# Two three-bank score tiles that both lend a bank, one shared bank, and a second temporary for the scan's output weights

## Chip, cores and metric

The kernel runs on one core of one Trainium2 chip. The metric is the device time in microseconds of one execution; before the change three runs gave a median of 770.16 us (769.84 to 772.17).

## What is computed

Two independent blocks over 2048 positions of width 640, joined along the last axis. Block A is a diagonal complex state space: the input is projected to 640 complex states, a linear recurrence runs over the positions, and the states are projected back with a skip term. Block B is attention with 32 query heads of 20 columns that share one head of keys and one of values, without a mask, followed by an output projection.

```
# A
Bu = x @ B_bar.T            # complex, 2048 x 640
h[t] = Lam_bar * h[t-1] + Bu[t]
y = 2 * real(h @ C.T) + x * Dskip
# B
scores = (x wq)_h . (x wk) * 20**-0.5      # 32 heads, 2048 x 2048 each
o = softmax(scores) @ (x wv)
out = concat(y, o @ wo)
```

## The kernel before

Almost all of the time goes into the exponentials of the scores. The work is cut into units: one head, 512 queries and 128 keys give a score tile of 128 partitions by 512 columns, which is one PSUM bank. Four heads and 512 queries are a group (32 groups, 64 units each, 2048 units in all). A unit is made by PE (QK: `R<-QT,KT` or `B<-QT,KT`), turned into bf16 weights, and multiplied with the values and a column of ones into the bank PV (`PV<-P,VP` or `PV<-Pd,VP`).

The exponential has two makers. ACT reads a whole tile of several banks in one activation (L1263, P<-R). DVE takes single units: one instruction adds an offset and rounds to int16 (L1269, Pd<-B or Pd<-R), which as bits of bf16 approximates a power of two, and three shifted copies (L1274, over up to three units at once) correct it, so that a unit of DVE has four PV products where one of ACT's has one.

PSUM has eight banks. Before, tile R0 has three banks, tile R1 two, PV one, and two banks, B0 and B1 (tensor BB), are shared. ACT works on R0 and R1 in turn while PE fills the other. A unit for DVE goes to B0 or B1 or, with `lend`, to R0's third bank R0c; then R0's next tile has two banks. The shared banks also serve the background, each piece of which locks a bank from its first matmul until DVE has read it: the scan's input (thread sa: five matmuls, then L901), its output y (sy: 12 or 13 matmuls, L962), the dense Q (qt: five matmuls, L775, with the norm row at L800), and the output projection (proj: five matmuls, L1061).

The order on each engine is fixed when the program is built. A planner (`main`) holds a clock for each engine and modelled durations, gathers in every round the next operation of each thread and the next fill, exponential, DVE unit, shift and PV step, gives each its earliest start plus a bias, and issues the smallest. Small random choices of its thresholds (`vary`) change 64 times in the course, by the numbers in SEEDS. A fill is ordered ahead of a background matmul that would make it late (`t_fill`, with `after` for how late it may be). If PE would wait more than SPARE, the planner adds matmuls by zeros into PV that keep PE's clock up. `want_d` says whether a unit for DVE is wanted: DVE's backlog must be small, the bank free, and no background thread starved; lending ends when 40 units of the last group are taken (`t_left`).

The scan runs in units of 512 positions and 128 states (20 in all): L901 makes rotated inputs (tm), POOL adds them (uh, L917), DVE scans (L928), POOL rotates back (tm<-hh) and writes W (W<-tm), and PE turns W into y with the output weights CGre and CGim. Those weights are made once: the C matrices arrive by transposing DMAs in W's memory (Craw) and ostage; for each of ten products POOL multiplies five pieces into the temporary ctmp (L858), then DVE combines them (L860). Before, there is one ctmp, inside tm, and the scan's way back waits for all ten (`prog["c"]`). The dense part for 512 queries (L1011, OTd) reads the heads' outputs back from DRAM and normalises them.

P, ACT's output, is a ring of ten tile places with 25 units. The set-up (0 to about 22 us) makes K from four banks, of which it holds two while V is made (`rest`).

Of the kernel before, what the change touches and what calls it, by code (L numbers as in the profile page):

```python
# [243 lines left out]
class _Kernel:  # L244
    S, D, H, DH = 2048, 640, 32, 20
    NC, NQB, NKC, NGG = 5, 4, 16, 8
    BANKS = 2
    PIECES = "abcd"
    TILES, PTILES, DUNITS, DSHIFT, QRING = (3, 2), 10, 9, 3, 4
    SHIFTS = (0, 33, 65, 95)  # L250

# [3 lines left out]
    SPARE = 0.33  # L255
# [9 lines left out]
    SEEDS = (19006, 20002, 21006, 22006, 23001, 24003, 25001, 26002, 27008, 28003, 0, 30006, 31008, 32005, 33006,  # L265
# [28 lines left out]
    def alloc(self):  # L294
        S, NC = self.S, self.NC
        nc = self.nc
        self.R = [self.scope.enter_context(nc.psum_tensor(f"R{i}", [128, 512 * n], FP32))
                  for i, n in enumerate(self.TILES)]
        self.PV = self.scope.enter_context(nc.psum_tensor("PV", [128, 512], FP32))
        self.BB = self.scope.enter_context(nc.psum_tensor("B", [128, 512 * self.BANKS], FP32))  # L300
        self.B = [self.BB[:, 512 * i:512 * i + 512] for i in range(self.BANKS)] + [self.R[0][:, 1024:1536]]
        self.bkeys = [f"B{i}" for i in range(self.BANKS)] + ["R0c"]
        self.p.psum.update(["R0", "R0c", "R1", "R1b", "PV", *(f"B{i}" for i in range(self.BANKS))])
# [25 lines left out]
        self.sb("P", [128, self.PTILES * 5 // 2, 512], BF16)  # L329
# [7 lines left out]
        self.wq_raw = self.P[:].rearrange("p s n -> p (s n)")[:, 18 * 512:18 * 512 + NC * 640].rearrange("p (c n) -> p c n", c=NC)  # L337
# [24 lines left out]
        self.ctmp = self.tm[:].rearrange("p i n -> p (i n)").bitcast(FP32)[:, 1024:1664]  # L362
# [67 lines left out]
    def setup(self):  # L430
# [51 lines left out]
        pk = ["P7", "P8", "P9"]  # L482
# [23 lines left out]
        banks = [(K.R[1], 0, "R1"), (K.R[1], 512, "R1b"), (K.BB, 0, "B0"), (K.BB, 512, "B1")]  # L506
# [39 lines left out]
        for m, src, keys in ((0, K.R[1][:, 0:1024], ["R1", "R1b"]), (1, K.BB[:, 0:1024], ["B0", "B1"])):  # L546
# [270 lines left out]
    def scan_ops(self):  # L817
# [4 lines left out]
        sa, su, sr, sy, sc_ = [], [], [], [], []  # L822
        self.prog = prog = dict(x=0, a=0, u=0, s=0, r=0, y=0, w=0, c=0)
# [9 lines left out]
        ct = [f"tm{i}{h}" for i in (4, 5, 6) for h in self.PIECES]  # L833
# [14 lines left out]
        for c in range(NC):  # L848
            for i, nm in ((0, "cre"), (1, "cim")):
                sc_.append(self.dma(K.Craw[c][:, i, :], t[nm][:, 128 * c:128 * (c + 1)], f"craw{c}{i}",  # L850
                                    writes=[f"Craw{c}{i}"] + ([f"ostage{i}"] if c == 4 else []), tr=True, kb=160))
        for c in range(NC):
            cr, ci = K.Craw[c][:, 0, :], K.Craw[c][:, 1, :]
            keys = [f"Craw{c}0", f"Craw{c}1", "sc"] + (["ostage0", "ostage1"] if c == 4 else ws)
            for (dst, x, y, gx, gy, op, nm) in ((K.CGre, cr, ci, GRE, GIM, ALU.subtract, "CGre"),
                                                (K.CGim, ci, cr, NGRE, NGIM, ALU.add, "CGim")):
                for i in range(0, 640, 128):
                    pool(lambda e, y=y, c=c, gy=gy, i=i: e.tensor_scalar(K.ctmp[:, i:i + 128], y[:, i:i + 128], sc[:, gy, c:c + 1],  # L858
                                                                         None, op0=ALU.mult), keys, [f"ct{i}"] + ct * (i == 0), 128)
                dve(lambda e, dst=dst, x=x, op=op, c=c, gx=gx: e.scalar_tensor_tensor(  # L860
                    out=dst[:, c, :], in0=x, scalar=sc[:, gx, c:c + 1], in1=K.ctmp, op0=ALU.mult, op1=op),
                    keys + ct + [f"ct{i}" for i in range(0, 640, 128)], [nm], 695)
        sc_[-1].done = lambda: prog.update(c=1)
# [16 lines left out]
        sx = [o for b in (1, 2, 3) for o in self.load_xa(b, lambda b=b: prog["y"] >= 4 * (b - 1), lambda b=b: prog.update(x=b))]  # L880
        return sc_, sy, sr, su, sa, sx
# [7 lines left out]
    def scan_in(self, ops, dve, b, c):  # L889
# [4 lines left out]
        for k, (nm, BT) in enumerate((("BTre", K.BTre), ("BTim", K.BTim))):  # L894
            h = Hold()
            for cd in range(NC):
# [5 lines left out]
                K.tm[:, 2 * k:2 * k + 2, :], bass.AP(tensor=K.BB, offset=512 * int(h.key[1]),  # L902
# [224 lines left out]
    def main(self):  # L1127
# [184 lines left out]
        while True:  # L1312
# [108 lines left out]
            if kind == "bg":  # L1421
# [5 lines left out]
                if o.free:  # L1427
                    owner[int(o.hold.key[1])] = None
# [102 lines left out]
```

## Time and profile before

| | us |
|---|---|
| median of three runs | 770.16 |
| the profiled execution | 770.28 |
| its span, first to last instruction | 768.6 |
| ACT busy in the span | 752.5 |
| DVE busy | 708.3 |
| PE busy (pipelined, ends modelled) | 704.8 |
| POOL busy | 446.0 |

The profile is one execution on the chip. Its page gives busy times by engine, the chain of work that ended last, and groups of instructions by line with output and input tile, count, busy time, mean duration, and the idle time before them with what ended it. All PE work is recorded at one helper line (L421), so PE is read by tiles. The granted clock (PEclk) is the share of full speed that the chip's throttle gave to PE.

### The profile page before, as it was taken

To read this page: it belongs to the slowest core of one execution; us is meant where nothing else is said; L and a number is where in the kernel's file an instruction comes from. 1 tells how busy PE (TensorE), PEld (TensorE's weight loads), DVE (VectorE), ACT (ScalarE), POOL (GpSimd) and SP (SyncE) were. 2 spreads that over 40 slices of the span, in tenths; PEclk is the share of its full clock that TensorE was granted. 3 is DMA by queue.
4 is the path that set the end of the run, shared out by engine and by line. 5 is a ranking of instruction groups with operands and counts; after the bars stand their busy time and mean duration, and the time that the engine had idled before them with its cause. 6 is when DMAs were issued, how large, how long until landed. Compare 5 with 4: busy or idle time off the path is not lost.

```text
span 768.6 us, 16664 instructions
## 1 busy us (share of the span) xinstructions
PE 704.8 (92%) x6538; PEld 213.4 (28%) x6538; DVE 708.3 (92%) x1236; ACT 752.5 (98%) x710; POOL 446.0 (58%) x867
## 2 busy tenths in 40 slices
PE   5799988888889999998889999988889999889998
PEld 2222222222222333322223323322223332223333
DVE  5599999999998999999997999999999789999986
ACT  8999999999999999999999999999999999999995
POOL 5612354579989931088997300199986469990040
PEclk9899999899999999999999999999999999999999
DMA  9366301000021100220002100040000201000020
GB/s 186 57 143 134 74 16 49 8 24 14 3 51 30 42 8 27 56 60 15 15 9 67 42 23 9 23 93 10 15 15 28 66 33 34 14 15 17 18 61 35
DMA packets 61179, 31.50 MB, mean 41 GB/s; under 512 B 41510, under 2 KB 61102, under 8 KB 61102
## 3 DMA queue, kind: packets, MB, share of 16 engines
q1 hardware_dynamic: 59606, 30.14, 15.9%
q8 instruction: 52, 0.85, 0.5%
q10 hardware_dynamic: 1496, 0.30, 0.2%
q14 instruction: 25, 0.20, 0.1%
HBM read 9.21 MB, written 12.69 MB: 28 GB/s over the span
## 4 chain that ended last, share of the span: by engine, by line
ACT 74%; PE 15%; DVE 9%; POOL 1%; DMA 1%; issue 1%; ACTq 0%; DVEq 0%; POOLq 0%
ACT P L1263 72%; PE R L421 5%; PE PV L421 5%; PE B L421 4%; DVE Pd L1274 4%; DVE Pd L1269 3%; DVE hh L928 1%; DVE tm L901 1%; POOL tm L858 1%; DMA WO<-in_B_wk_dram 1%; ACT cs L691 1%; ACT Pd L690 0%; ACT KT L538 0%; DVE CGre L860 0%; ACT L503 0%
## 5 line engine op out<-in xcount | busy, mean ns | idle before, releaser
L1263 ACT ACTIVATE P<-R 128x1024 bf16<-128x1024 f32 (+1 forms) x677 | 733.1, 1354 | 4.3 <-PE R L421 1.8
L421 PE MATMUL R<-QT,KT 32*128 32x512 bf16 (+1 forms) x1685 | 266.9, 389 | 48.6 <-ACT P L1263 37.1
L1269 DVE TENSOR_SCALAR Pd<-B 128x512 int16<-128x512 f32 x363 | 245.5, 682 | 19.4 <-PE B L421 17.0
L1274 DVE TENSOR_SCALAR Pd<-Pd 128x1536 int16<-128x1536 int16 (+2 forms) x513 | 260.2, 541 | 0.4
L421 PE MATMUL PV<-Pd,VP 128*32 128x512 bf16 x1744 | 256.9, 386 | 2.0 <-DVE OTr L1307 1.0
L421 PE MATMUL PV<-P,VP 128*32 128x512 bf16 x1612 | 253.3, 389 | 0.7 <-DVE OTr L1307 0.6
L917 POOL TENSOR_TENSOR tm<-hh,cs 128x128 bf16<-128x128 f32 x320 | 163.9, 533 | 17.7 <-DVE hh L928 8.3
L421 PEld LDWEIGHTS R<-QT,KT 32*128 32x128 bf16 (+1 forms) x1685 | 66.1, 91 | 301.0 <-ACT P L1263 271.0
L421 PE MATMUL B<-QT,KT 32*128 32x512 bf16 x363 | 141.0, 389 | 0.0
L917 POOL TENSOR_TENSOR uh<-tm 128x128 bf16<-128x128 bf16 x160 | 81.0, 527 | 97.6 <-DVE tm L901 93.7
L917 POOL TENSOR_TENSOR W<-tm 128x128 bf16<-128x128 bf16 x160 | 93.5, 608 | 49.4 <-PE B L421 45.3
L421 PEld LDWEIGHTS PV<-Pd,VP 128*32 128x32 bf16 x1744 | 60.1, 94 | 65.7 <-issue 40.5
L421 PEld LDWEIGHTS PV<-P,VP 128*32 128x32 bf16 x1612 | 58.1, 94 | 58.8 <-issue 46.6
L1011 POOL TENSOR_TENSOR OTd<-OTd,rwide 128x128 bf16<-128x128 bf16 x80 | 33.2, 443 | 60.0 <-DMA OTd<-o_rows 58.2
L1269 DVE TENSOR_SCALAR Pd<-R 128x512 int16<-128x512 f32 x73 | 49.9, 683 | 3.0 <-PE R L421 2.4
L901 DVE TENSOR_TENSOR tm<-B,cs 128x1024 bf16<-128x1024 f32 x40 | 48.5, 1213 | 1.0 <-PE B L421 0.6
L858 POOL TENSOR_SCALAR tm<-W,sc 128x128 f32<-128x128 bf16 x40 | 32.3, 821 | 27.5 <-DVE CGre L860 15.9
L421 PE MATMUL B<-CGre,W 128*128 128x384 bf16 (+1 forms) x160 | 46.4, 305 | 0.0
L421 PE MATMUL B<-CGim,W 128*128 128x384 bf16 (+1 forms) x160 | 45.5, 299 | 0.0
L928 DVE TENSOR_TENSOR_SCAN hh<-sc,hini,uh 128x512 f32<-128x512 f32 x30 | 40.7, 1358 | 0.0
L421 PEld LDWEIGHTS B<-QT,KT 32*128 32x128 bf16 x363 | 32.9, 91 | 0.0
L421 PE MATMUL B<-xaT,BTre 128*128 128x512 bf16 x100 | 30.1, 384 | 0.1
(149 smaller groups left out, 437.2 us busy)
## 6 DMA issues: line engine op xcount, KB each, us to landing
o_rows<-OTr SPq DMA_DIRECT2D x32, 128.0 KB, 1.7
QT<-q_rows SPq DMA_DIRECT2D x30, 128.0 KB, 2.2
q_rows<-Qd SPq DMA_DIRECT2D x16, 160.0 KB, 2.9
OTd<-o_rows SPq DMA_DIRECT2D x16, 160.0 KB, 3.4
out_dram<-ystage SPq DMA_DIRECT2D x16, 160.0 KB, 1.9
out_dram<-ostage SPq DMA_DIRECT2D x12, 160.0 KB, 1.8
P<-in_B_wq_dram SPq DMA_DIRECT2D x1, 800.0 KB, 5.6
WO<-in_B_wo_dram SPq DMA_DIRECT2D x4, 200.0 KB, 3.4
```

The source lines that it names most:

```text
L421: ins = e.matmul(o() if callable(o) else o, lhsT=l, rhs=r, start=st, stop=sp, skip_group_check=True, **kw)
L691: act(lambda e, c=c, b=b: e.activation(K.cs[:, c, :, :].rearrange("p i n -> p (i n)"), K.tri[:, 4 * b + 2:4 * b + 4, :].rearrange("p r n - ...
L858: pool(lambda e, y=y, c=c, gy=gy, i=i: e.tensor_scalar(K.ctmp[:, i:i + 128], y[:, i:i + 128], sc[:, gy, c:c + 1], None, op0=ALU.mult), key ...
L901: dve(lambda e, k=k, h=h: e.tensor_tensor(K.tm[:, 2 * k:2 * k + 2, :], bass.AP(tensor=K.BB, offset=512 * int(h.key[1]), ap=[[512 * self.BA ...
L917: put(lambda e, c0=c0, end=end: e.tensor_tensor(out[:, c0:end], a[:, c0:end], b[:, c0:end], op), reads, [writes + h], n, gate=None if i el ...
L928: dve(lambda e, ri=ri, ini=ini: e.tensor_tensor_scan(K.hh[:, ri, :], dec, K.uh[:, ri, :], ini, ALU.mult, ALU.add), ["sc", *(f"uh{ri}{h}" f ...
L1011: ops.append(Op("pool", lambda e, c=c, m=m: e.tensor_tensor(K.OTd[:, m, c], K.OTd[:, m, c], K.rwide[:, c], ALU.mult), rw + [f"OTe{dd}" for ...
L1263: return Op("act", lambda e: e.activation(dst, K.R[n % 2][:, 0:512 * size], ACT.Exp, scale=self.exp_scale), [f"R{n % 2}"] + ["R0c"] * (siz ...
L1269: return Op("dve", lambda e: e.tensor_scalar(K.Pd[:, 0, u, :], K.B[x][:, :], self.d_off, 0.0, op0=ALU.add, op1=ALU.max), [key], [f"Pd{u}_0 ...
L1274: return Op("dve", lambda e: e.tensor_scalar(K.Pd[:, i, a:b, :], K.Pd[:, 0, a:b, :], float(self.SHIFTS[i]), 0.0, op0=ALU.subtract, op1=ALU ...
```

## The change

PSUM becomes R0 (three banks), R1 (three banks), PV and one shared bank B0; R1 and B0 are one tensor, RB. Both tiles lend their third bank (R0c, R1c) to a unit of DVE. All of the background locks B0. P's ring hands out places unit by unit. The planner gets new random knobs: `prefer` lends even where B0 is free, `gap` spaces the blocks of one background thread, and the allowed lateness of a fill (`after`) goes by whether the tile that ACT has next is three wide. While the set-up's end runs and no PV matmul has begun, idle matmuls of the identity into B0 fill waits of PE over 0.25 us (WARM). The output weights get two temporaries in OTd and threads of their own (sl: loads, sk: POOL, sg: DVE); now only the writing of W and the dense part wait for them, the way back's rotations do not. The C loads stand ahead of wo's, and xa's second block waits for three of the ten products. All seeds are new.

```
-    BANKS = 2
+    BANKS = 1
-    TILES, PTILES, DUNITS, DSHIFT, QRING = (3, 2), 10, 9, 3, 4
+    TILE, PUNITS, DUNITS, DSHIFT, QRING = 3, 25, 9, 3, 4
-    SPARE = 0.33
+    SPARE, WARM = 0.33, 0.8
...
+        self.R0 = self.scope.enter_context(nc.psum_tensor("R0", [128, 512 * self.TILE], FP32))
+        self.RB = self.scope.enter_context(nc.psum_tensor("R1", [128, 512 * (self.TILE + 1)], FP32))
+        self.R = [self.R0, self.RB[:, 0:512 * self.TILE]]
+        self.B = [self.RB[:, 1536:2048], self.R[0][:, 1024:1536], self.R[1][:, 1024:1536]]
+        self.bkeys = ["B0", "R0c", "R1c"]
...
-        self.ctmp = self.tm[:].rearrange("p i n -> p (i n)").bitcast(FP32)[:, 1024:1664]
+        self.ctmp = self.OTd[:].rearrange("p c n -> p (c n)").bitcast(FP32).rearrange("p (i n) -> p i n", i=2)
...
+                    wide(lambda e, y=y, c=c, gy=gy, i=i, h=h: e.tensor_scalar(K.ctmp[:, h, i:i + 128], y[:, i:i + 128], sc[:, gy, c:c + 1],
+                                                                            None, op0=ALU.mult), keys, [f"ct{h}{i}"], 128,
+                         gate=lambda n=2 * c + h: prog["g"] >= n - 1 and prog["l"] > n // 2, done=(lambda n=2 * c + h + 1: prog.update(k=n)) if i == 512 else None)
+                cd(lambda e, dst=dst, x=x, op=op, c=c, gx=gx, h=h: e.scalar_tensor_tensor(
+                    out=dst[:, c, :], in0=x, scalar=sc[:, gx, c:c + 1], in1=K.ctmp[:, h, :], op0=ALU.mult, op1=op),
...
+        sx = [o for b in (1, 2, 3) for o in self.load_xa(b, lambda b=b: prog["y"] >= 4 * (b - 1) and prog["g"] > 2, lambda b=b: prog.update(x=b))]
...
-                   gate=lambda: prog["s"] > u and prog["c"], done=(lambda: prog.update(r=u + 1)) if i == 3 else None)
-        free = lambda: prog["y"] >= 4 * b
+                   gate=lambda: prog["s"] > u, done=(lambda: prog.update(r=u + 1)) if i == 3 else None)
+        free = lambda: prog["y"] >= 4 * b and prog["c"]
...
-        have = lambda: all(g in self.normed for g in range(self.NGG * qb, self.NGG * qb + (6 if qb == self.NQB - 1 else 8))) and (
+        have = lambda: self.prog["c"] and all(g in self.normed for g in range(self.NGG * qb, self.NGG * qb + (6 if qb == self.NQB - 1 else 8))) and (
...
-        self.lend = r.choice((0.5, 1.0))
-        self.open, self.first = r.choice((0.6, 0.7)), r.choice(("sy", "proj", None))
+        self.lend, self.prefer = r.choice((0.0, 0.5, 1.0)), r.choice((False, True))
+        self.gap = dict(sy=r.choice((0.0, 4.0, 8.0)), proj=r.choice((0.0, 4.0, 8.0)), sa=r.choice((0.0, 0.0, 4.0)),
+                        qt=r.choice((0.0, 0.0, 4.0)))
+        self.open, self.first = r.choice((0.6, 0.7, 0.8)), r.choice(("sy", "proj", None))
...
-            f = [i for i in range(2) if owner[i] is None]
-            if not f:
-                return None
-            return min(f, key=lambda i: p.begin("pe", (), (f"B{i}",)))
+            return 0 if owner[0] is None else None
...
-                    size, x = self.TILES[n % 2] - (n % 2 == 0 and owner[2] is not None), bank(None)
+                    lent = 1 + n % 2
+                    size, x = self.TILE - (owner[lent] is not None), bank(None)
                     d = want_d(g, t, n % 2)
-                    if not d and size == 3 and want_d(g, t, 0, True):
-                        size, d, x = 2, True, 2
+                    if (not d or self.prefer) and size == 3 and want_d(g, t, 0, lent):
+                        size, d, x = 2, True, lent
...
-                    t_fill = (t_fill, t_fill + self.after[n % 2])
+                    t_fill = (t_fill, t_fill + self.after[bool(tiles) and len(tiles[-1][1]) == 3])
...
+                    if o.lock and t_left() and not (name == "qt" and not self.qsent):
+                        bias += max(0.0, last.get(name, -99.0) + self.gap.get(name, 0.0) - p.clock["pe"])
...
+                if self.still and not any(begun[0]) and owner[0] in (None, "rest") and "B0" not in o.keys()[1]:
+                    while t - p.begin("pe", (), ("B0",)) > 0.25 and self.load(t) < self.WARM:
+                        self.go(self.mms([self.m1(K.B[0], K.ident[:, :], K.xbT[:, 0, 0:512], True, True)], ["ident", "xbT0"], ["B0"],
+                                         kind="zero"))
```

More of the change, by code (lines that the diff above doesn't have):

```diff
@@ new lines, in scan_ops @@
+        old = ["wk4", "wk_raw", "wv_raw", "onesrow", "selrow"] + ["veclim", "vecldt", "veclre", "vecdsk"]
+        sk, sg = [], []
+        cd = mk(sg, "dve")
+        wide = lambda fn, reads, writes, n, **k: sk.append(Op("pool", fn, reads, writes, occ=0.58, **k))
+        for c in range(NC):
+            cr, ci = K.Craw[c][:, 0, :], K.Craw[c][:, 1, :]
+            keys = [f"Craw{c}0", f"Craw{c}1", "sc"] + (["ostage0", "ostage1"] if c == 4 else ws)
+            for (dst, x, y, gx, gy, op, nm) in ((K.CGre, cr, ci, GRE, GIM, ALU.subtract, "CGre"),
+                                                (K.CGim, ci, cr, NGRE, NGIM, ALU.add, "CGim")):
+                h = int(nm == "CGim")
+                for i in range(0, 640, 128):
+                    wide(lambda e, y=y, c=c, gy=gy, i=i, h=h: e.tensor_scalar(K.ctmp[:, h, i:i + 128], y[:, i:i + 128], sc[:, gy, c:c + 1],
[3 more added lines that the diff above has]
+                    out=dst[:, c, :], in0=x, scalar=sc[:, gx, c:c + 1], in1=K.ctmp[:, h, :], op0=ALU.mult, op1=op),
+                    keys + [f"ct{h}{i}" for i in range(0, 640, 128)], [nm] + [f"OTd{i}{j}" for i in range(NC) for j in self.PIECES] * (c == NC - 1), 695,
+                    gate=lambda n=2 * c + h: prog["k"] > n, done=lambda n=2 * c + h + 1: prog.update(g=n, c=int(n == 2 * NC)))
@@ L847, in scan_ops @@
                 sc_.append(self.dma(dst, src, f"wo{j}{w}", reads=["WO4"], writes=[f"WO4_{j}{w}"], kb=200 if w else 50))
[L848 to L863, printed above, removed]
         for b in range(4):
@@ L1245, in fill_op @@
         def fill_op(n, out, d, x):
-            lst, reads, writes = [], set(), ([f"R{n % 2}"] if out else []) + ["R0c"] * (len(out) == 3)
+            lst, reads, writes = [], set(), ([f"R{n % 2}"] if out else []) + [f"R{n % 2}c"] * (len(out) == 3)
             units = list(out) + ([d] if d else [])
@@ L1345, in main @@
                             offer("fill", fill_op(n, [], d, bank(None)), 0.2, arg=([], d, bank(None)))
-            full = bool(tiles) and tile_left.get(tiles[0][0] - self.PTILES, 0) > 0
+            full = bool(tiles) and not vacant(len(tiles[0][1]))
             if tiles:
                 n, out = tiles[0]
-                if tile_left.get(n - self.PTILES, 0) == 0:
+                if not full:
                     offer("ex", ex_op(n, len(out)), 0.0)
@@ L1426, in main @@
                     since.pop(name, None)
+                    last[name] = p.clock["pe"]
                 if o.free:
```

85 lines of the change are left out of this document (46 added, 39 removed), and 8 rows, old and new, of the table SEEDS.

## The prediction

> **What bounds the kernel now.** I read the page first: the engines' busy times, then the chain that ended last.
>
> ```profile
> span 768.6 us, 16664 instructions
> PE 704.8 (92%) x6538; PEld 213.4 (28%) x6538; DVE 708.3 (92%) x1236; ACT 752.5 (98%) x710; POOL 446.0 (58%) x867
> ...
> PEclk9899999899999999999999999999999999999999
> ...
> ACT 74%; PE 15%; DVE 9%; POOL 1%; DMA 1%; issue 1%; ACTq 0%; DVEq 0%; POOLq 0%
> ```
>
> ACT is busy 98% of the span and is most of the chain. To see what else the span holds, I cut it at ACT's first and last exponential with the windows view (columns: length, then busy us and count of PE, PEld, DVE, ACT, POOL, then clock, DMA share, GB/s).
>
> ```profile
> 0.00:21.68 21.68, 12.65 (x43) 4.45 (x43) 12.82 (x29) 17.96 (x32) 11.81 (x30) 1.00 0.82 166
> 21.68:757.80 736.12, 684.72 (x6413) 204.68 (x6417) 691.00 (x1198) 731.87 (x679) 434.14 (x838) 0.99 0.15 37
> 757.80:768.60 10.80, 7.45 (x86) 4.30 (x78) 4.45 (x11) 2.65 (x4) 0.00 (x0) 1.00 0.17 61
> ```
>
> In the middle 736.12 us ACT works 731.87 and idles 4.25. All stalls together are thus worth 4.25 us; anything larger must come from ACT's own work: how many score units it gets, and how many instructions they are packed into. The groups with shapes kept apart show both (count, then busy us, mean ns).
>
> ```profile
> L1263 ACT ACTIVATE P<-R 128x1024 bf16<-128x1024 f32 x419 | 457.8, 1189 | 1.1 <-PE R L421 0.7 <-PE B L421 0.2
> L1263 ACT ACTIVATE P<-R 128x1536 bf16<-128x1536 f32 x258 | 418.3, 1621 | 3.2 <-PE R L421 1.2 <-PE B L421 1.1 <-PE PV L421 0.6
> L421 PE MATMUL PV<-P,VP 128*32 128x512 bf16 x1612 | 253.3, 389 | 0.7 <-DVE OTr L1307 0.6
> L421 PE MATMUL PV<-Pd,VP 128*32 128x512 bf16 x1744 | 256.9, 386 | 2.0 <-DVE OTr L1307 1.0 <-DVE Pd L1274 0.5 <-DVE Pd L1269 0.4
> L1269 DVE TENSOR_SCALAR Pd<-B 128x512 int16<-128x512 f32 x363 | 245.5, 682 | 19.4 <-PE B L421 17.0
> L1269 DVE TENSOR_SCALAR Pd<-R 128x512 int16<-128x512 f32 x73 | 49.9, 683 | 3.0 <-PE R L421 2.4
> ```
>
> ACT takes 1612 units of 512 columns (419 x 2 + 258 x 3 = 1612), DVE the other 363 + 73 = 436 (1744 / 4). Neighbouring exponentials overlap, so the two busy figures add to more than the union; that union is in the page's groups:
>
> ```profile
> L1263 ACT ACTIVATE P<-R 128x1024 bf16<-128x1024 f32 (+1 forms) x677 | 733.1, 1354 | 4.3 <-PE R L421 1.8
> L1274 DVE TENSOR_SCALAR Pd<-Pd 128x1536 int16<-128x1536 int16 (+2 forms) x513 | 260.2, 541 | 0.4
> ```
>
> One bank more costs 1621 - 1189 = 432 ns. With 677 tiles, 677a + 258 x 0.432 = 733.1, so a two-bank tile takes a = 0.918 us of ACT's time, of which two banks are 0.864. **A tile costs 0.054 us beyond its banks**; a unit costs 733.1 / 1612 = 0.455 us. These two prices carry the forecast: 0.054 for each tile less, about 0.45 for each unit that moves to or from DVE.
>
> **The change part by part.** *Wider tiles.* Both tiles now have three banks, and either lends its third to DVE; only one bank, B0, is left for the background (scan, projections, dense Q) and DVE's units together. A tile is two wide where it lends. So I need how many of DVE's units find B0 free. Its use by the background comes from the view of tile B (first and last start after the durations), and, for a projection, from the timeline (start, length):
>
> ```profile
> L421 PE MATMUL B<-CGre,W x160: 272/304/337, 267.4 to 740.7; 128*128 128x384 bf16 x80, 128*128 128x256 bf16 x80
> L421 PE MATMUL B<-xaT,BTre x100: 376/379/390, 55.1 to 657.1; 128*128 128x512 bf16 x100
> L901 DVE TENSOR_TENSOR tm<-B,cs x40: 1192/1212/1225, 57.3 to 661.2; 128x1024 bf16<-128x1024 f32 x40
> L962 DVE CAST ystage<-B x32: 408/474/558, 270.7 to 741.7; 128x384 bf16<-128x384 f32 x16, 128x256 bf16<-128x256 f32 x16
> ...
> 434.87 0.72 PE L421 MATMUL B<-WO,OTd 128*128 128x320 bf16 x4
> ...
> 436.45 0.48 DVE L1061 CAST ostage<-B 128x320 bf16<-128x320 f32 x1
> ```
>
> The first scan input holds a bank from 55.1 to 57.3 + 1.21, 3.4 us; the first half row of y from 267.4 to 270.7 + 0.56, 3.9; a projection from 434.87 to 436.93, 2.1. With 40 scan inputs, 32 y halves, 28 projections and 20 dense-Q blocks (five matmuls as a scan input and a shorter evacuation; I take 2.9), that is 136 + 125 + 59 + 58 = 378 us of the 725 us in which there are DVE units: an estimate that B0 is free 48% of the time. If DVE takes units at an even rate, 0.48 x 436 = 209 come from B0 and 227 are lent. With some 5 more two-wide tiles at the start there are 232, then (1612 - 464) / 3 = 383 three-wide ones: 615 tiles, 62 fewer, **-3.3 us**. The bounds: all 436 lent gives 441 two-wide, 243 three-wide, 7 tiles more, +0.4; none lent gives about 541 tiles, -7.3. I take the value from the free share.
>
> By the Trainium skill, ScalarE: Activation LUTs, section What ACT_TABLE_LOAD costs, an ACTIVATE with immediate operands takes 186 ns + 0.833 ns per column, and neighbours overlap by about 93 ns. By it a tile costs 93 ns beyond its banks and the 62 tiles 5.8 us; the rows above give 54 ns, and the measurement decides.
>
> *DVE's share.* DVE has three banks to draw from before (two shared, one lent) and after (one shared, two lent), but the background can no longer take two at once. What more units could come is in DVE's waits from 48 to 740 us (total, times, longest):
>
> ```profile
> DVE Pd L1269 <- PE B L421: 14.9, 53, 0.7
> DVE ystage L962 <- PE B L421: 7.2, 7, 2.1
> ...
> DVE Pd L1269 <- PE R L421: 2.4, 7, 0.7
> ```
>
> DVE stood 17.3 us waiting for a unit's scores. A unit costs DVE (245.5 + 49.9 + 260.2) / 436 = 1.27 us, so these waits are 13.6 units. With the 7.2 us before y's evacuation it would be 19.3, -8.8 us: the far end; the near one is 0, and what lies below nothing is the third rival. Nothing in the trace prices it more closely; I take a third of the 13.6, 4.5 units x 0.455 = **-2.1 us**. Against it: lending stops in the last group once 40 of its 64 units are taken, and there B0 is shared with the last projections. The timeline has six of DVE's units there, these first and last, out of two banks; I take two off (between none and six), **+0.9 us**.
>
> ```profile
> 746.83 0.69 DVE L1269 TENSOR_SCALAR Pd<-B 128x512 int16<-128x512 f32 x1 [0.34 <-PE B L421]
> ...
> 755.87 0.69 DVE L1269 TENSOR_SCALAR Pd<-B 128x512 int16<-128x512 f32 x1
> ```
>
> *Idle matmuls.* They keep PE's clock up in the set-up, into B0, until the first PV matmul:
>
> ```profile
> 28.00:34.00 6.00, 5.59 (x23) 1.11 (x27) 0.83 (x3) 5.83 (x6) 2.12 (x10) 0.52 0.05 5
> ...
> 22.07 2.18 PE L421 MATMUL PV<-WO,xbT 128*128 128x20 bf16 x80
> ...
> 24.62 9.21 ACT L1263 ACTIVATE P<-R 128x1536 bf16<-128x1536 f32 x8 [0.58 <-PE R L421]
> 34.45 14.20 ACT L1263 ACTIVATE P<-R 128x1536 bf16<-128x1536 f32 x13 [0.62 <-PE PV L421]
> ```
>
> The granted clock from 28 to 34 us is 0.52, and ACT's second gap there, 0.62 us at 34.45, stands behind PV matmuls on the slow clock. The first gap, at 24.62, has the fill behind V's 80 matmuls, before the clock falls, and stays. I take **-0.6 us**, between -1.2 (both gaps) and +0.4 (a 0.39 us matmul just ahead of a late fill). An idle matmul stands in PE's queue before whatever comes next, so if PE's wait is shorter than planned, the fill and then ACT wait for it.
>
> *Output weights of the scan.* The same 50 POOL and 10 DVE instructions; two temporaries in OTd in place of one in tm, so POOL need not wait for DVE to release it:
>
> ```profile
> POOL tm L858 <- DVE CGre L860: 20.3, 5, 8.4
> ...
> POOL tm L858 <- DVE CGim L860: 16.0, 4, 5.7
> ...
> 82.97 1.27 SPq L402 DMA_TRANSPOSE ostage<-in_A_C_re_dram  x1
> ...
> 162.75 8.10 POOL L917 TENSOR_TENSOR tm<-hh,cs 128x128 bf16<-128x128 f32 x16 [1.02 <-DVE CGim L860]
> ...
> 741.70 0.42 DVE L962 CAST ystage<-B 128x256 bf16<-128x256 f32 x1
> ...
> L421 PE MATMUL B<-WO,OTd x140: 297/299/310, 242.0 to 756.0; 128*128 128x320 bf16 x140
> ...
> L404 SPq DMA_DIRECT2D OTd<-o_rows x16: 316/436/465, 226.7 to 736.9; - x16
> ```
>
> The scan's way back starts at 162.75 us, behind those weights, and its last y leaves at 741.70, 16 us ahead of the last exponential's start. Starting earlier is worth nothing on ACT: 0. The ten C transposes move ahead of wo's loads on SP's queue (1.27 us each, 13 us). Q's rows share that queue but the planner prefers them, and wo is first used at 242 us, so this hides; without that preference a group's Q could come up to 13 us late. The new gate on xa's second block stands on the same queue; scan units of that block come after five of the first. OTd is first loaded at 227 us, so the dense part's new gate costs nothing while the weights finish before it.
>
> *P's ring, lateness by tile, gaps between background blocks, new seeds.* The ring holds the same 25 units. The rest moves waits about; all of ACT's waits left are 4.25 - 0.6 us, so I take 0, between -3.6 and +4.
>
> **Sum.** The profiled execution took 770.28 us (span 768.6 and 1.7 around it), 0.1 over the median of 770.16. 770.28 - 3.3 - 2.1 + 0.9 - 0.6 = **765.2 us**, 0.6% less.
>
> **The rivals.** *One: DVE's gaps close.* With a lendable bank at every fill DVE gains all 19.3 units, -8.8 in place of -2.1: 758.5. For it: ACT is the chain and its other costs are fixed. Against: DVE already works 691 of 736 us.
>
> *Two: nothing comes of it.* Background holds and preferred lending leave B0 hardly a unit, so two-wide tiles stay near 419, and DVE's count stays: 770.3 - 0.6 = 769.7. For it: 73 of 436 units are lent now, and the plan may lend even where B0 is free. It decides where over 400 units are lent.
>
> *Three, slower: DVE starves at the one shared bank.* A background block keeps B0 some 2 to 4 us, and a lent bank only comes free when DVE has read it; where DVE is behind, the next tile of the same kind is two wide and can't lend. Each unit that DVE loses costs ACT 0.455 us. Of the gains 3.3 + 0.6 = 3.9 us would be left, so it decides from 9 fewer units on (9 x 0.455 = 4.1); with 20 fewer it is 770.3 - 3.9 + 9.1 = 775.5. For it: B0 would be nearly always taken. Against: the two lendable banks are there at every fill.
>
> *Four, slower: PE's clock falls more often.* Fewer, wider tiles are fewer passes on PE. This happened once in the middle:
>
> ```profile
> 140.00:143.00 3.00, 2.15 (x19) 0.49 (x15) 3.00 (x7) 3.00 (x4) 2.73 (x5) 0.64 0.16 52
> 143.00:146.00 3.00, 3.00 (x21) 0.56 (x17) 2.17 (x6) 2.48 (x3) 0.51 (x1) 0.50 0.00 0
> 146.00:149.00 3.00, 3.00 (x28) 0.67 (x27) 2.98 (x6) 2.40 (x3) 0.36 (x1) 0.72 0.00 0
> ```
>
> PE works 2.15 of 3 us, the clock drops to 0.50, and ACT then idles 0.52 + 0.60 = 1.1 us. Seven such dips more would make it about 773. The planner still fills gaps over 0.33 us with matmuls into PV. The Trainium skill, TensorE: Matmul & The Clock Gate, section A second HAM failure mode: psum-queue depth-cycling, speaks for this rival: cycling through PSUM banks leaves short idle times in which the clock oscillates; the page's row of the clock above agrees so far that it fell in two stretches.
>
> **Chances.** The forecast's course (762 to 768) 0.50; one 0.18; two 0.12; three 0.14; four 0.06. A measurement of this kernel tells about 0.3%, 2.3 us, from no change. Faster by more: 0.50 + 0.18 = 0.68; within it: 0.12; slower: 0.20. For 8 times in 10 I leave out what goes beyond rival one and the worse half of three: 757.5 to 774.
>
> **What would show it.** Three-wide exponentials near 383 and two-wide near 232, in all near 615; the lent count (Pd from R) near 227 and Pd from B near 209, together near 440; ACT's idle time in the middle near 4 us; the clock from 28 to 34 us near 1; POOL's waits for CGre and CGim gone. Wrong if DVE's units change by more than ten either way, or if new waits on ACT exceed 4 us.

## The result and the profile after

The changed kernel takes 773.61 us (median of six runs, 772.79 to 774.03); the kernel before, run beside it, 769.72 (six runs, 768.84 to 772.17). The ratio is 1.0053, with an interval of 1.0037 to 1.0068: **slower by half a per cent**, where 765.2 and faster was forecast. The profiled executions took 773.55 and 770.28, so what the two traces show, 3.2 us of span, is most of the 3.9.

The page of the changed kernel, in the lines that answer to those of before:

```profile
span 771.8 us, 16662 instructions
PE 698.8 (91%) x6526; PEld 212.8 (28%) x6526; DVE 706.5 (92%) x1214; ACT 754.3 (98%) x696; POOL 443.7 (57%) x867
...
PEclk9699999999999999999999999999999999999999
...
ACT 81%; PE 6%; DVE 6%; POOL 4%; issue 1%; DMA 0%; ACTq 0%; POOLq 0%; DVEq 0%
```

ACT is the bound as before, and it works 1.8 us more. In this execution PE's clock falls once, in the second slice, and not again before the end. Which work ACT has is in the groups with shapes kept apart (count, then busy us, mean ns, then idle time before):

```profile
L1278 ACT ACTIVATE P<-R 128x1536 bf16<-128x1536 f32 x293 | 434.2, 1633 | 3.0 <-PE R L422 2.7
L1278 ACT ACTIVATE P<-R 128x1024 bf16<-128x1024 f32 x370 | 382.1, 1210 | 2.8 <-PE R L422 2.5
L1284 DVE TENSOR_SCALAR Pd<-R 128x512 int16<-128x512 f32 x429 | 289.0, 683 | 30.4 <-PE R L422 26.0
```

and in the page's own group, where neighbouring exponentials are a union:

```profile
L1278 ACT ACTIVATE P<-R 128x1024 bf16<-128x1024 f32 (+1 forms) x663 | 735.0, 1397 | 5.8 <-PE R L422 5.2
```

There are 663 tiles, 14 fewer than before (677), where 62 fewer were forecast; DVE has 429 units, 7 fewer (436); ACT so has 370 x 2 + 293 x 3 = 1619, 7 more (1612). What the span gained is then read from rows alone. The exponentials' union grew from 733.1 to 735.0, +1.9, and ACT's idle time ahead of them from 4.3 to 5.8, +1.5. The first and the last exponentials, after and then before:

```profile
21.08 2.41 ACT L1278 ACTIVATE P<-R 128x1536 bf16<-128x1536 f32 x2
...
748.45 13.42 ACT L1278 ACTIVATE P<-R 128x1536 bf16<-128x1536 f32 x10
```

```profile
739.72 19.32 ACT L1263 ACTIVATE P<-R 128x1024 bf16<-128x1024 f32 x18
```

They begin 0.6 us sooner (21.08 against 21.68); behind the last one lie 771.80 - 761.87 = 9.93 us where there were 768.60 - 759.04 = 9.56, +0.4. 1.9 + 1.5 - 0.6 + 0.4 = 3.2, the whole difference of the spans. By the prediction's own prices, 7 units more are 7 x 0.455 = +3.2 us and 14 tiles fewer 14 x 0.054 = -0.8, together 2.4 for the measured 1.9.

**Where the third banks went.** All banks but PV go by one tile name now (B0 is a part of the tensor R1). In experiment idle_short, which keeps the changed kernel's order of work, units out of lent banks (L1285) and out of B0 (L1284) are recorded at lines of their own:

```profile
L1285 DVE TENSOR_SCALAR Pd<-R 128x512 int16<-128x512 f32 x357 | 240.9, 683 | 21.7 <-PE R L422 17.6
...
L1284 DVE TENSOR_SCALAR Pd<-R 128x512 int16<-128x512 f32 x72 | 49.1, 682 | 10.3 <-PE R L422 9.8
```

357 of 429 units are lent, 72 come from B0. Of 370 two-wide tiles, 357 are two wide because they lent. Before, 73 were lent and 363 came from two shared banks.

**Where the seven units went.** DVE's units by stretch (length, DVE's busy us and count, clock, DMA share, GB/s), after and then before:

```profile
21.08:48.00 26.92, 5.86 (x9) 0.75 0.53 90
48.00:200.00 152.00, 53.95 (x81) 1.00 0.21 49
200.00:750.00 550.00, 227.76 (x337) 1.00 0.11 32
```

```profile
21.68:48.00 26.32, 6.00 (x10) 0.87 0.48 86
48.00:200.00 152.00, 66.08 (x99) 0.97 0.22 51
200.00:750.00 550.00, 219.25 (x325) 1.00 0.11 31
```

Six of the seven are lost between 48 and 750 us (418 for 424): 18 up to 200 us, of which 12 come back later. In the early stretch DVE now has twelve steps of the scan (L934) where it had six (L928), and the scan's way back starts at 90.9 us in place of 162.8. The whole of DVE from 48 to 750 us (length, then busy us and count of PE, PEld, DVE, ACT, POOL, then clock, DMA share, GB/s), after and then before:

```profile
48.00:750.00 702.00, 643.41 (x6097) 193.00 (x6085) 664.41 (x1127) 699.52 (x635) 416.19 (x800) 1.00 0.13 35
```

```profile
48.00:750.00 702.00, 653.63 (x6106) 194.59 (x6099) 664.31 (x1139) 699.09 (x647) 420.02 (x803) 0.99 0.14 36
```

DVE is busy 664.41 us for 664.31, so it idles no longer than before. What it waits for has changed, though (48 to 740 us; total, times, longest), after and then before:

```profile
DVE Pd L1284 <- PE R L422: 23.2, 58, 2.1
PE R L422 <- DVE Pd L1284: 8.3, 16, 1.3
...
PEld R L422 <- DVE Pd L1284: 6.1, 17, 1.6
...
ACT P L1278 <- PE R L422: 2.1, 4, 0.8
```

```profile
PEld B L421 <- DVE Pd L1269: 9.3, 35, 0.4
...
PE R L421 <- DVE Pd L1269: 3.2, 8, 0.8
...
ACT P L1263 <- PE R L421: 1.3, 4, 0.6
ACT P L1263 <- PE B L421: 1.3, 4, 0.5
```

DVE's wait for a unit's scores is 23.2 us, where it was 14.9 + 2.4 = 17.3: 5.9 us more. But its 7.2 us of waits ahead of y's evacuation are gone, and the two about cancel. In the same busy time DVE did six units fewer; why, the trace doesn't show. A part may be that its 366 shifts of three units took 620 ns each, where they took 608, 4.4 us in all. PE's waits for DVE's reads, 14.4 against 12.5, and ACT's waits, 2.1 against 2.6, hardly moved here.

**Where ACT's stalls grew.** At the start, in ACT's timeline of the changed kernel from 24 to 42 us and in PE's windows (length, PE's busy us and count, clock, DMA share, GB/s):

```profile
24.55 2.37 ACT L1278 ACTIVATE P<-R 128x1536 bf16<-128x1536 f32 x2 [1.06 <-PE R L422]
27.23 2.36 ACT L1278 ACTIVATE P<-R 128x1536 bf16<-128x1536 f32 x2 [0.32 <-PE R L422]
30.06 3.02 ACT L1278 ACTIVATE P<-R 128x1536 bf16<-128x1536 f32 x2 [0.46 <-PE R L422]
33.94 1.45 ACT L1278 ACTIVATE P<-R 128x1536 bf16<-128x1536 f32 x1 [0.86 <-PE R L422]
35.76 6.52 ACT L1278 ACTIVATE P<-R 128x1024 bf16<-128x1024 f32 x7 [0.38 <-PE R L422]
```

```profile
18.10:21.50 3.40, 1.53 (x8) 1.00 0.04 11
21.60:25.00 3.40, 3.40 (x86) 0.50 0.74 172
25.00:28.40 3.40, 3.34 (x11) 0.50 0.02 5
28.40:31.85 3.45, 3.39 (x17) 0.50 0.06 5
31.85:35.25 3.40, 3.40 (x16) 0.50 0.13 16
35.25:38.65 3.40, 3.38 (x30) 1.00 1.24 181
```

Five gaps, 3.08 us, where before there were two, 0.58 + 0.62 = 1.20. PE is busy almost throughout, on half the clock, from 21.6 to 35.25 us. Before, the clock was down only from 28.2 to 35.0 there.

### The profile page after: what moved, and what is told of

It reads as the page before. It is cut to its first block, busy times and chain, and to the rows that moved or that the text cites. A ratio compares the mean times of both kernels' runs of the same rounds, so it can differ in the third digit from the quotient of the medians.

```text
span 771.8 us, 16662 instructions
## 1 busy us (share of the span) xinstructions
PE 698.8 (91%) x6526; PEld 212.8 (28%) x6526; DVE 706.5 (92%) x1214; ACT 754.3 (98%) x696; POOL 443.7 (57%) x867
## 4 chain that ended last, share of the span: by engine, by line
ACT 81%; PE 6%; DVE 6%; POOL 4%; issue 1%; DMA 0%; ACTq 0%; POOLq 0%; DVEq 0%
ACT P L1278 79%; PE R L422 5%; DVE Pd L1289 2%; POOL OTd L852 2%; DVE Pd L1284 2%; PE PV L422 2%; POOL tm L923 1%; POOL uh L923 1%; ACT cs L692 1%; DVE hh L934 1%; DVE tm L907 0%; ACT Pd L691 0%; DVE Qd L776 0%; DMA WO<-in_A_Lambda_im_dram 0%; ACT KT L539 0%
## 5 line engine op out<-in xcount | busy, mean ns | idle before, releaser
L1278 ACT ACTIVATE P<-R 128x1024 bf16<-128x1024 f32 (+1 forms) x663 | 735.0, 1397 | 5.8 <-PE R L422 5.2
L1284 DVE TENSOR_SCALAR Pd<-R 128x512 int16<-128x512 f32 x429 | 289.0, 683 | 30.4 <-PE R L422 26.0
L422 PE MATMUL R<-QT,KT 32*128 32x512 bf16 x2048 | 261.6, 386 | 57.6 <-ACT P L1278 40.9
L422 PEld LDWEIGHTS R<-QT,KT 32*128 32x128 bf16 x2048 | 66.4, 91 | 303.1 <-ACT P L1278 273.1
L907 DVE TENSOR_TENSOR tm<-R,cs 128x1024 bf16<-128x1024 f32 x40 | 48.3, 1208 | 1.1 <-PE R L422 0.8
L422 PE MATMUL R<-CGre,W 128*128 128x384 bf16 (+1 forms) x160 | 46.6, 305 | 0.0
L422 PE MATMUL R<-CGim,W 128*128 128x384 bf16 (+1 forms) x160 | 45.6, 299 | 0.0
L852 POOL TENSOR_SCALAR OTd<-W,sc 128x128 f32<-128x128 bf16 x40 | 32.0, 809 | 14.5 <-DMA W<-in_A_C_im_dram 10.2
L934 DVE TENSOR_TENSOR_SCAN hh<-sc,hini,uh 128x512 f32<-128x512 f32 x30 | 40.2, 1344 | 0.0
L422 PE MATMUL R<-WO,OTd 128*128 128x320 bf16 x160 | 30.2, 302 | 0.5 <-issue 0.3
L422 PE MATMUL R<-xaT,BTre 128*128 128x512 bf16 x100 | 30.1, 384 | 0.4 <-DVE Pd L1284 0.2
L422 PE MATMUL R<-xaT,BTim 128*128 128x512 bf16 x100 | 29.6, 384 | 0.1
```

The lines of the kernel that those rows point to most:

```text
L422: ins = e.matmul(o() if callable(o) else o, lhsT=l, rhs=r, start=st, stop=sp, skip_group_check=True, **kw)
L852: wide(lambda e, y=y, c=c, gy=gy, i=i, h=h: e.tensor_scalar(K.ctmp[:, h, i:i + 128], y[:, i:i + 128], sc[:, gy, c:c + 1], None, op0=ALU.mu ...
L907: dve(lambda e, k=k, h=h: e.tensor_tensor(K.tm[:, 2 * k:2 * k + 2, :], bass.AP(tensor=K.RB, offset=1536, ap=[[2048, 128], [0, 2], [1, 512] ...
L934: dve(lambda e, ri=ri, ini=ini: e.tensor_tensor_scan(K.hh[:, ri, :], dec, K.uh[:, ri, :], ini, ALU.mult, ALU.add), ["sc", *(f"uh{ri}{h}" f ...
L1278: return Op("act", lambda e: e.activation(dst, K.R[n % 2][:, 0:512 * size], ACT.Exp, scale=self.exp_scale), [f"R{n % 2}"] + [f"R{n % 2}c"] ...
L1284: return Op("dve", lambda e: e.tensor_scalar(K.Pd[:, 0, u, :], K.B[x][:, :], self.d_off, 0.0, op0=ALU.add, op1=ALU.max), [key], [f"Pd{u}_0 ...
```

## The experiments

My theory after the result: the third banks that were to widen the tiles nearly all go to DVE, because the one shared bank is mostly taken, by the background or by the unit before; so tiles hardly widen, DVE loses some units on the way, and the start loses a little more on the slow clock. Rivals: the idle matmuls cost it; the new seeds are simply worse luck; the scan's part costs it; a lent bank costs by itself, whoever uses the shared one.

### The idle matmuls and the clock at the start

**idle_short**: the idle matmuls stream one column in place of 512, all else in the same order; units out of B0 have a line of their own. The edits here and below are shortened.

```
-  self.m1(K.B[0], K.ident[:, :], K.xbT[:, 0, 0:512], True, True)
+  self.m1(K.B[0][:, 0:1], K.ident[:, :], K.xbT[:, 0, 0:1], True, True)
```

> The changed kernel in its own order, but each idle matmul of the set-up streams 1 column instead of 512. Theory (the idle matmuls stand in the way of fills while the clock is low): the clock stays 0.50 from about 22 to 35 us, ACT's gaps at 27.2 and 30.1 us (0.32 and 0.46 us) go, and the time falls by 0.5 to 1.0 us, from 773.6 to about 772.8. Rival (the idle matmuls lie in PE's free time): time within 0.3 us of 773.6 and the gaps stay. Rival two (they hold up the clock a little): slower by up to 1 us.

773.09 us (769.05 before on that chip), ratio 1.0054 (1.0035 to 1.0073). The gaps at 27.23 and 30.06 are gone, and the clock comes back some 2.5 us sooner; the time doesn't tell it from the changed kernel.

**idle_dense**: the idle matmuls get dense weights (a block of x) in place of the identity.

```
-  self.m1(K.B[0], K.ident[:, :], K.xbT[:, 0, 0:512], True, True)
+  self.m1(K.B[0], K.xbT[:, 1, 0:128], K.xbT[:, 0, 0:512], True, True)
```

> The changed kernel in its own order, but the idle matmuls' weights are 128 columns of x instead of the identity. If the clock stays low because an identity is too little activity, it is back at 1.00 by about 29 us and the time falls by about 1 us. If what fits into PE's waits at half clock is too little whatever the weights are, the clock is 0.50 until about 35 us as in the changed kernel and the time stays within 0.3 us of 773.6.

773.40, ratio 1.0057 (1.0038 to 1.0075). PE's windows:

```profile
22.00:25.00 3.00, 3.00 (x87) 2.35 (x85) 3.00 (x5) 2.37 (x2) 3.00 (x3) 0.52 0.36 67
25.00:28.00 3.00, 2.24 (x10) 0.52 (x8) 2.23 (x8) 2.36 (x2) 2.94 (x4) 0.50 0.39 92
28.00:34.00 6.00, 5.94 (x30) 1.26 (x27) 1.24 (x4) 5.17 (x5) 2.84 (x13) 0.64 0.11 31
```

The clock is down from 22 us on here too, and back some 3 us sooner than in the changed kernel, as in idle_short. So in these traces dense weights do no more for it than a single column.

**more_spin**: the set-up's last seven spins (matmuls whose result isn't used, which the kernel has up to 21 us already) are sent twice each.

```
-  [self.m1(K.R[0][:, 0:512], K.wk4[:, 0, :], K.xbT[:, 0, 0:512], True, True)]
+  [self.m1(K.R[0][:, 0:512], K.wk4[:, 0, :], K.xbT[:, 0, 0:512], True, True)] * more
```

> The changed kernel in its own order, but each of the last seven spin matmuls of the set-up (ahead of the first fills, from about 16 to 20 us) is sent twice, which fills some 1.5 us of the stretch in which PE idles before the clock falls at 21.6 us. Theory (the clock is lost in that idle stretch, and idle matmuls can then not bring it back): the clock stays 1.00 past 25 us, ACT's gaps between 27 and 36 us (2.0 us in all) mostly go, time about 772. Rival (the clock falls because of V's 80 small matmuls, as it did after them in the kernel before): it falls at about 25 us instead, gaps mostly stay, time 773 to 774.

774.28 (772.04 to 777.04), ratio 1.0064 (1.0042 to 1.0085). PE's windows, and ACT's timeline:

```profile
18.10:21.50 3.40, 3.25 (x18) 1.00 0.35 125
21.60:25.00 3.40, 3.15 (x90) 1.00 0.69 155
```

```profile
24.54 36.18 ACT L1281 ACTIVATE P<-R 128x1536 bf16<-128x1536 f32 x33 [0.40 <-PE R L422]
```

In this execution PE is busy 3.25 us of the stretch ahead of V's matmuls, not 1.53, the clock holds at 1.00, and ACT's timeline shows one unbroken run from 24.54 to beyond 60 us. That fits the theory that the clock is lost in PE's idle stretch before 21.6 us and that matmuls put in behind come too late. One trace doesn't prove it: the kernel before is as idle from 18 to 21 us (1.57 of 3.00) and kept its clock there, and the mean clocks of the six executions with more spins, 0.987 to 0.998, overlap with the changed kernel's, 0.987 to 0.996. The 772 us that were expected did not come either. In the trace the last exponential ends 1.1 us sooner (760.78), but a stall at 118 us lasts 1.32 us in place of 0.85, and the span goes on 3.9 us behind the last store's issue where it went on 2.2.

None of the three kernels differs from the changed one by more than the runs scatter, so what the idle matmuls stream is not where the 3.9 us went. Nor is it the mean clock: of the executions on that chip with a mean clock of 0.993, three of the kernel before took 768.15 to 768.24 us, and one each of idle_short, idle_dense and more_spin 772.67, 773.31 and 773.16.

### Is it the seeds?

All seeds are new, and each set was chosen for its kernel. **zero_before** and **zero_after** are the two kernels with every seed 0; **zero_after_free** is zero_after with the planner's restraint taken out: a unit takes B0 even if a background thread is starved, and a bank is lent only where B0 can't be had.

```
-    SEEDS = (...)
+    SEEDS = (0,) * 64
...   zero_after_free alone:
-            if any(t - x > self.starved[name] * (name != "qt" or len(self.qsent) > 0) for name, x in since.items()):
-                return False
-                    if (not d or self.prefer) and size == 3 and want_d(g, t, 0, lent):
+                    if not d and size == 3 and want_d(g, t, 0, lent):
```

> The kernel before with all 64 seeds 0, so that no choice of the planner's thresholds is fitted to its layout. Theory (the layout with one shared bank is what costs, and its seeds hide most of that): this one loses some 15 to 25 us against its own 769.7, to about 790, with the background done before the last exponential. Rival (the layouts are alike and after has worse seeds): the same loss as the changed layout has with seeds 0.

> The changed kernel with all seeds 0. Theory (the background queues for the one shared bank): the last exponential ends at about 785, not far from that of the kernel before with seeds 0, but scan, y and projections go on behind it, and the span is about 815, some 25 us over the kernel before with seeds 0. Rival (the layouts are alike): within 8 us of the kernel before with seeds 0, and the last exponential is followed by 10 us as now.

> The changed kernel with all seeds 0 and two edits to the planner: a background thread that has waited no longer keeps units for DVE off the shared bank, and a unit is lent a tile's third bank only where the shared one isn't to be had. Theory (tile width and background compete for that bank): over 115 units in the shared bank and some 650 tiles, the last exponential about 10 us earlier than with seeds 0 alone, but the background ends later, the span about 835. Rival (the bank has room, as the forecast's 48% had it): about 200 units in the shared bank, about 620 tiles, and a span below that with seeds 0 alone.

One execution each: 788.80, 807.17 and 832.85 us. In zero_after 355 units are lent and 71 come from B0, the changed kernel's split almost to the unit, with other seeds. In zero_after_free:

```profile
L1279 DVE TENSOR_SCALAR Pd<-R 128x512 int16<-128x512 f32 x301 | 203.1, 684 | 19.0 <-PE R L418 16.0
L1278 DVE TENSOR_SCALAR Pd<-R 128x512 int16<-128x512 f32 x131 | 89.6, 684 | 32.3 <-PE R L418 30.9
```

131 units out of B0 (L1278), 301 lent, 651 tiles. Its last exponential ends sooner than zero_after's (773.16 against 777.65 us), but behind it lie 57.7 us where zero_after has 27.8 and zero_before 11.4: the background had been kept from the bank and had to be done at the end. B0 goes either to DVE or to the background; the 4.5 us that wider tiles gain here are lost several times over at the end.

**eq_before** and **eq_after** have seeds found by the same short search (512 plans from zeros), so that neither has the longer one. The edit is the SEEDS line alone.

> The kernel before with seeds from a short search of its own: from all 0, turn by turn, the best of 8 choices by the planner's own clock. It is the yardstick of the next three, which got the same search. Both theories expect some 7 us over 769.7, about 777, since the search is short.

> The changed kernel with seeds from the same short search. Theory (the layout with one shared bank costs, whatever the seeds): 3 to 5 us over the kernel before with the same search, about 781, with about 74 units in the shared bank and 667 tiles. Rival (the 3.9 us between the two kernels are luck of their seeds): within 2 us of it, either side.

780.00 (ratio to before 1.0151, 1.0130 to 1.0172) and 785.36 (1.0215, 1.0196 to 1.0234): the changed kernel is 5.4 us behind at equal search. That speaks against bad luck with the seeds, but it is one search for each, and the changed planner has more choices to search. What it loses looks different, too: DVE's units are level here (431 and 433), DVE idles 41.9 of the 702 us from 48 to 750 where eq_before's idles 37.9, and ACT waits more. Waits of eq_after and of eq_before:

```profile
ACT P L1274 <- PE R L418: 13.7, 27, 1.9
```

```profile
ACT P L1259 <- PE B L417: 6.2, 12, 1.6
...
ACT P L1259 <- PE R L417: 2.9, 4, 1.4
```

13.7 against 9.1 us of ACT's waits for scores. The change is paid for in units with the one set of seeds and in stalls with the other. The clock has a share in those stalls that isn't parted off: it was 0.975 to 0.985 in the four executions of eq_after and 0.987 to 0.989 in eq_before's, and executions of the kernel before on one chip took 767.77 us at 0.996 and 771.49 at 0.986.

### One part alone

**eq_before_cg** is the kernel before with only the scan's part of the change (two temporaries, own threads, the gates), **eq_after_nowarm** the changed kernel without idle matmuls, each with seeds searched as above.

```
eq_before_cg, on before:
-        self.ctmp = self.tm[:].rearrange("p i n -> p (i n)").bitcast(FP32)[:, 1024:1664]
+        self.ctmp = self.OTd[:].rearrange("p c n -> p (c n)").bitcast(FP32).rearrange("p (i n) -> p i n", i=2)
...
eq_after_nowarm, on the changed kernel:
-    SPARE, WARM = 0.33, 0.8
+    SPARE, WARM = 0.33, 0.0
```

> The kernel before with the one part on the scan's output weights (two temporaries in OTd, own threads, its gates) and seeds from the same short search. Theory (that part is off the path): within 2 us of the kernel before with the same search, with the weights done near 110 us in place of 162 and y done earlier. Rival (DVE's ten products, now early, push units for DVE to ACT where the background is thin): 3 us or more slower.

> The changed kernel without the idle matmuls of the set-up, with seeds from the same short search. Theory (they bring nothing that can be measured): within 2 us of the changed kernel with the same search. Rival (they are what slows it, through the plan that reckons with a warm PE): 3 us or more faster, level with the kernel before with the same search.

781.21 (1.0161, 1.0140 to 1.0182), level with eq_before within the intervals: alone, the scan's part shows no worth either way. But DVE has 425 units there, six fewer than in eq_before, and 80 from 48 to 200 us where eq_before has 90: the same loss in the same stretch as in the changed kernel. 782.48 for the other, but its four runs go from 779.32 to 789.77 (1.0192, 1.0127 to 1.0258): between eq_before and eq_after, and it settles nothing.

### Without y in the shared bank

**noy_before** and **noy_after** leave out the scan's output y (that half of the output isn't computed), and with it 114 of the 392 us for which the background holds B0 in the changed kernel; seeds are searched as above for each.

```
-                self.y_tile(sy, mk(sy, "dve"), b, q)
+                sy.append(Op("dve", lambda e: e.memset(K.ystage[:, 0:8], 0.0), self.w_keys, ["ystage"], ...))     # once a block
```

> The kernel before without the scan's output y: the 128 matmul groups into the shared banks, their evacuations and the stores of block A's half of the output are left out (that half is not computed), which takes some 125 us of holds off the shared banks and as many us off PE. Seeds searched from zeros over 512 plans, as for eq_before. Both theories expect it faster than eq_before's 780.0, about 765 to 776, with DVE's units near 439. It is the base line of noy_after.

> The changed kernel without y, seeds searched alike. Theory (the one shared bank is contended by the background): with a third of the background's holds gone some 150 units, twice the count of eq_after, find it free, tiles fall to about 636, and the layout's cost of 5.4 us at equal search (eq_after against eq_before) vanishes: noy_after against noy_before between -4 and +1 us. Rival (a lent bank costs by itself: the next fill waits until DVE has read it, whoever else uses the shared bank): the cost stays, +3.5 to +6 us.

772.31 (1.0042, 1.0026 to 1.0058) and 774.82 (1.0074, 1.0055 to 1.0094): 2.5 us apart, neither gone nor kept, and with these intervals the difference to the 5.4 above isn't certain either. The groups say more. Of noy_after, then of noy_before:

```profile
L1273 ACT ACTIVATE P<-R 128x1536 bf16<-128x1536 f32 x338 | 499.0, 1592 | 8.8 <-PE R L418 8.6
L1273 ACT ACTIVATE P<-R 128x1024 bf16<-128x1024 f32 x298 | 320.7, 1163 | 1.7 <-PE R L418 1.4
```

```profile
L1258 ACT ACTIVATE P<-R 128x1024 bf16<-128x1024 f32 x399 | 445.5, 1207 | 3.0 <-PE B L417 1.5 <-PE R L417 1.4
L1258 ACT ACTIVATE P<-R 128x1536 bf16<-128x1536 f32 x270 | 440.4, 1631 | 3.5 <-PE R L417 2.4 <-PE PV L417 0.6 <-PE B L417 0.3
```

With y gone the tiles do widen: 338 three-wide ones against 270, and with 298 two-wide ones at most 298 of its 437 units were lent, so at least 139 found B0, about twice the changed kernel's 72 (with other seeds). That is the theory's half. But the 33 tiles saved are worth 33 x 0.054 = 1.8 us, and ACT's idle time is 10.5 against 6.5 us, mostly ahead of three-wide tiles, while PE waits longer for DVE's reads:

```profile
PE R L418 <- DVE Pd L1279: 10.7, 27, 1.0
PEld R L418 <- DVE Pd L1279: 10.5, 30, 1.0
```

21.2 us, where noy_before has 12.7 in its three rows of that kind. That speaks for the rival's half: a bank that is lent must be read by DVE before it can be filled again, and this costs though B0 is freer. But the clock is lower too (mean 0.969 against 0.982; both have less work for PE), so how much of the 4 us of ACT's idle time are DVE's reads isn't shown.

## Why the prediction was wrong

The step that failed is **"an estimate that B0 is free 48% of the time ... 209 come from B0 and 227 are lent"**. Its first half held: counted in the trace from a background piece's first matmul to the end of DVE's read, B0 is held 392 us in the changed kernel; 378 were estimated, without the norm row, which holds it 29. The second half doesn't follow from it. A free share isn't a share of fills that find the bank free. DVE's own unit holds it for at least a matmul and a read, 0.386 + 0.683 = 1.07 us by the rows, and for 1.47 on average over the 363 units out of B0 and B1 in the kernel before, from the matmul's start to the read's end; a fill comes each 740.8 / 663 = 1.12 us. At 1.47 us B0 serves every second fill at best. The other 333 us between the background's pieces lie in 123 gaps, only 48 of them over 1.5 us; units of 1.47 us, packed one behind the other, would fit into them some 170 times. That it was 72 lies in part with the planner's order, which keeps the bank for a background thread that waits and may lend even where B0 is free: with both taken out, zero_after_free got 131 in place of 71, and paid for it at the end. So 72 came from B0, 357 were lent, and 14 tiles were saved: -0.8 us for the -3.3 forecast. Rival two said that this could be, "hardly a unit from B0", and set its mark at 400 lent; its time, 769.7, missed the rest. Of the prediction's own signs, the counts of tiles and of lent units show the error; its two marks for being wrong (DVE's units by more than ten, ACT's new waits over 4 us) were not reached.

The step **"DVE's share"** had the wrong sign: +3.2 us for -1.2. I took a third of DVE's 17.3 us of waits as units to come; those waits became 23.2, DVE's idle time as a whole stayed, and seven units were lost. The two units that I took off for the ban on lending did go: behind the 2024th of the 2048 score matmuls DVE begins to read four units before the change and two after it (counted in the traces; the prediction had six). In number this is near rival three, just short of its own mark (9 units), and it was enough, since of the 3.9 us of gains that the mark reckons with only 0.8 came. But rival three's mechanism, a DVE that starves at the shared bank, is not shown in this pair, where DVE idles no longer; in eq_after it idles 4.0 us longer than in eq_before and loses no units. At least three causes are left for the seven units and not separated: the bank itself, the scan's work that now falls into the stretch up to 200 us, and DVE's own pace (a shift of three units took 620 ns, 608 before).

**Idle matmuls**: -0.6 forecast, ACT's start stalls grew by 3.08 - 1.20 = 1.9 us. I had costed what they do to a clock that falls at 28 us; it fell at 21.6, ahead of them. Elsewhere ACT's stalls went from 3.1 to 2.7.

**Output weights of the scan**: 0 was forecast. POOL's ten products end 41 us sooner and the last y leaves 49 us sooner, and alone the part shows no gain or loss of time (eq_before_cg). DVE's six units fewer there are a term that the prediction put at nothing; what it is worth in the changed kernel stays open. The views of lines L852 and L968 (least, median and greatest ns, first and last start):

```profile
L852 POOL TENSOR_SCALAR OTd<-ostage,sc x10: 592/600/1737, 111.2 to 119.6; 128x128 f32<-128x128 bf16 x10
```

```profile
L968 DVE CAST ystage<-R x32: 390/476/558, 205.2 to 692.3; 128x384 bf16<-128x384 f32 x16, 128x256 bf16<-128x256 f32 x16
```

**Rival four** was wrong for this kernel: in its trace the clock, once back at 35.25 us, did not fall again before the end (mean 0.991, 0.989 before). The Trainium skill's page TensorE: Matmul & The Clock Gate, section A second HAM failure mode: psum-queue depth-cycling, tells of a clock that oscillates as PSUM banks are cycled; this trace doesn't show that.

**The price of a tile**, 0.054 us, could be larger. From the changed kernel's rows, 735.0 = 663a + 293 x (1.633 - 1.210) gives a = 0.922 us, less two banks of 0.423 each 0.076. The Trainium skill's page ScalarE: Activation LUTs, section What ACT_TABLE_LOAD costs, by whose 93 ns I had given a second sum, lies above both. It changes little: 14 tiles are 0.8 to 1.1 us.

What stays open: why DVE did seven units fewer, the largest term of the loss; how the rest parts between the bank, lending and the clock at the start; and whether a longer search could bring the new layout level. In all four pairs the changed layout was the slower one, by 3.9 us with its own seeds, 5.4 with the short search, 2.5 without y and 18.4 with seeds 0 (single executions). No kernel here beat the one before.

## What to carry to other kernels

A resource that is free half of the time isn't there for half of the requests: count the gaps that are long enough, the requester's own hold and the reserve kept for others, and ask how many requests can be served in a row. Before a loss is put down to one wait, look at the engine's whole idle time: here one wait grew and another went. When a buffer is turned from one use to two, price both uses out of the same bank; what a wide tile gives was here an eighth of what the unit that must move in its place costs (0.054 against 0.455 us). Where an order is searched for by seeds, compare layouts only at equal search, and over more than one search.

## What the runs showed that was not expected

Once PE's clock was down, keeping PE busy did not bring it back for a long time: in the changed kernel PE is busy 3.40, 3.34, 3.39 and 3.40 us of four stretches of 3.4 us at 0.50 (the ends of matmuls are modelled in a trace), and the clock is full only from 35.25 on, 13.65 us after the fall. The Trainium skill's page TensorE: Matmul & The Clock Gate, section The HAM clock gate (the "warmup" mystery), has it back after about 3.4 us of sustained work and speaks of a window of 3413 ns; the trace agrees with the window, since the stretches on half the clock in these runs' traces last 3.4, 6.8, 10.2, 13.65, 17.1, 20.5 or 23.9 us, all near multiples of it, and disagrees with the return. What differs between the busy stretches that lift the clock and those that don't, the runs don't show.
